# Attention with routed keys and an FFN: rounding the weights on VectorE alone, checking them in a second reading, and running the second block a few turns behind

## The chip, the cores and the metric

One core of a Trainium2 chip runs the kernel. The metric is device time in microseconds; for the kernel before, the median of three runs is 1088.34 us (1087.57 to 1089.61). Engines are named as the profile names them: PE is TensorE, PEld its weight load, DVE is VectorE, ACT is ScalarE, POOL is GpSimd, SP is the queue that issues the DMAs.

## The reference

Two blocks follow each other. The first is an attention with 4 batches, 8 heads, 768 positions and head size 64: each query and each key is given to the nearest of 16 centroids of its head, and a query attends only to keys of the same cluster. The second is an FFN on 3072 tokens with 512 inputs and 2048 hidden units.

```python
mask = q_assign[:, :, :, None] == k_assign[:, :, None, :]
scores = scale * np.matmul(q, k.transpose(0, 1, 3, 2))
scores = np.where(mask, scores, -1000000000.0)
attn = np.exp(scores - max); attn = attn / (attn.sum(-1) + 1e-09)   # in short
x = np.matmul(attn, v)            # (B,H,S,D) -> (B*S, H*D)
# ...
h = x @ w_in                      # 512 x 2048
g = h * (1.0 / (1.0 + np.exp(-1.702 * h)))
out = (g @ w_out).astype(np.float32)   # 2048 x 512
```

The FFN's weights come in as 64-bit floats: two 32-bit words for each number. The kernel reads them as words and makes 32-bit floats of them itself.

## The kernel before

The main loop has 96 turns (and two more to drain). A turn `t` works on two units of attention: scores (PE), for the first batch a matmul on one-hot clusters (`part`), `exps` (ACT), `mask` (DVE for the later batches, and the sums on POOL), and the `values` (PE) of the turn before. Twelve turns make half a batch, 24 a batch. Every third turn normalises a group; the fourth of these releases the FFN of that half batch, 28 chunks: 16 `first` (x times w_in, then tanh on ACT, then a product on DVE) and 12 `second` parts (g times w_out). Chunks are handed out by the turn.

The weights are 32 chunks of 128 x 512 numbers, 512 KB each as they come. Chunk by chunk they are rounded into `w_in` (16 chunks) and then `w_out` (16).

```python
def load_w(i):                       # SP; the raw words, three buffers
    if i < NW:
        t = wp.tile([P, WN, 2], I32, name="raw")
        nc.sync.dma_start(out=t.rearrange("p n t -> p (n t)"), in_=w_chunks[i][1])
        w_raw[i] = t

def split_w(i):                      # hi: the high words, every second one
    hi = w_raw[i][:, :, 1]; w = w_chunks[i][0]
    e = wp.tile([P, WN], I32, name="e")
    nc.vector.tensor_scalar(out=e, in0=hi, scalar1=EXP, scalar2=None, op0=ALU.bitwise_and)   # L159
    nc.vector.tensor_scalar(out=w.bitcast(I32), in0=hi, scalar1=0xFFFFF, scalar2=None,
                            op0=ALU.bitwise_and)                                             # L161
    nc.scalar.activation(out=e, in_=e, func=AF.Relu, scale=8.0, bias=low[:, 0:1])            # L163
    nc.scalar.activation(out=w, in_=w.bitcast(I32), func=AF.Copy, scale=2.0 ** -20, bias=1.0)# L165
    w_pow[i] = e

def join_w(i):
    raw, e, w = w_raw.pop(i), w_pow.pop(i), w_chunks[i][0]
    nc.vector.scalar_tensor_tensor(out=e, in0=raw[:, :, 1], scalar=-2 ** 31, in1=e, ...)     # L171
    nc.vector.scalar_tensor_tensor(out=w, in0=raw.bitcast(U32)[:, :, 0], scalar=2.0 ** -52,
                                   in1=w, op0=ALU.mult, op1=ALU.add)                         # L174
    nc.vector.tensor_tensor(out=w, in0=w, in1=e.bitcast(FP32), op=ALU.mult)                  # L177

def round_next():                    # splits a chunk, joins the one before
    i = w_done[0]
    if i < NW:
        load_w(i + 2)
        split_w(i)
    if 0 < i <= NW:
        join_w(i - 1)
    w_done[0] += 1
```

Normalising and its check, and the FFN:

```python
def normalise(g):
    sm = sum_of.pop(g); ps = bank()               # bank(): one of three PSUM banks
    # ... two pairs of matmuls with ones            L453
    rec = recs[g] = short()
    nc.vector.reciprocal(out=rec, in_=ps[:, 0:HALF])                                         # L456
    x = xT_of[g] = O_of.pop(g)
    nc.vector.tensor_tensor(out=x, in0=x, in1=rec, op=ALU.mult)                              # L458
    if g % HP == HP - 1:
        ffn.extend(ffn_chunks(g // HP))

def check(g):                        # ACT sums 1/sum, to see whether it is in range
    rec = recs.pop(g)
    nc.scalar.activation(out=rec, in_=rec, func=AF.Copy, accum_out=sums[:, 0, g:g + 1])      # L468
    nc.scalar.activation(out=rec, in_=rec, func=AF.Relu, ...)                                # L470

def first(f):
    round_to((f * P // WN + 1) * NCH)             # rounds what it needs, here and now
    ps = bank()
    # ... matmuls                                   L487
    g = hs[f] = gp.tile([P, HALF], FP32, name="g")
    nc.scalar.activation(out=g, in_=ps[:, 0:HALF], func=AF.Tanh, scale=0.851)                # L492
    nc.vector.scalar_tensor_tensor(out=g, in0=g, scalar=1.0, in1=ps[:, 0:HALF], ...)         # L494
```

The loop (TB is 24, a batch):

```python
rate = (NF + NH * (NF // 4)) / (TB / 2 - 0.5)
for t in range(NT + 2):
    # scores (L384), part (L398), exps (L409) of two units
    second = t >= TB // 2
    if second:
        round_next()
    # mask (L420; sums L430); prep_near (L276); values (L441) of the turn before
    owed = owed + rate if ffn else 0.0
    # normalise(g) in every third turn, other preparation of the next heads
    # (transposes L262, assignment L287-L316), check
    if second or t and t % 4 != 3:
        round_next()
    while owed >= 1 and ffn:
        ffn.popleft()()
        owed -= 1
    if second and t % 2:
        round_next()
# after the loop: the chunks that are left, and a flag for a fallback kernel
```

If a sum or a weight is out of range, a flag sends the work to a second, general kernel, which does not run with these inputs.

Of the kernel before, what the change touches and what calls it, by code (L numbers as in the profile page):

```python
# [2 lines left out]

# [35 lines left out]
def fast(  # L39
# [21 lines left out]
    nc = tc.nc  # L61
# [26 lines left out]
    xp = ctx.enter_context(tc.tile_pool(name="xp", bufs=HP + 2))  # L88
# [63 lines left out]
    EXP = 0x7FF00000  # L152

    def split_w(i):

        hi = w_raw[i][:, :, 1]
        w = w_chunks[i][0]
        e = wp.tile([P, WN], I32, name="e")
        nc.vector.tensor_scalar(out=e, in0=hi, scalar1=EXP, scalar2=None,  # L159
                                op0=ALU.bitwise_and)  # L160
        nc.vector.tensor_scalar(out=w.bitcast(I32), in0=hi, scalar1=0xFFFFF,  # L161
                                scalar2=None, op0=ALU.bitwise_and)
        nc.scalar.activation(out=e, in_=e, func=AF.Relu, scale=8.0,  # L163
                             bias=low[:, 0:1])
        nc.scalar.activation(out=w, in_=w.bitcast(I32), func=AF.Copy,  # L165
                             scale=2.0 ** -20, bias=1.0)
        w_pow[i] = e

    def join_w(i):
        raw, e, w = w_raw.pop(i), w_pow.pop(i), w_chunks[i][0]  # L170
        nc.vector.scalar_tensor_tensor(  # L171
            out=e, in0=raw[:, :, 1], scalar=-2 ** 31, in1=e,
            op0=ALU.bitwise_and, op1=ALU.bitwise_or)
        nc.vector.scalar_tensor_tensor(  # L174
            out=w, in0=raw.bitcast(U32)[:, :, 0], scalar=2.0 ** -52, in1=w,
            op0=ALU.mult, op1=ALU.add)
        nc.vector.tensor_tensor(out=w, in0=w, in1=e.bitcast(FP32),  # L177
                                op=ALU.mult)

    w_done = [0]  # L180

    def round_next():
        i = w_done[0]
        if i < NW:
            load_w(i + 2)
            split_w(i)
        if 0 < i <= NW:
            join_w(i - 1)
        w_done[0] += 1

    def round_to(n):
        while w_done[0] <= min(n, NW):
            round_next()
# [11 lines left out]
    low = const.tile([P, 1], FP32, name="low")  # L205
    nc.vector.memset(low, -896.0 * 2.0 ** 23)
# [10 lines left out]

    hot = const.tile([P, NJ * 4, 32], BF16, name="hot")
    nc.vector.memset(hot, 0.0)
    sums = const.tile([P, 2, 2 * NPAIR], FP32, name="sums")  # L220

# [829 lines left out]
```

## Time and profile before

| | before |
|---|---|
| median of three runs | 1088.34 us |
| span of the profiled run | 1087.3 us |
| mean granted TensorE clock | 0.990 |
| HBM read, written | 38.04 MB, 6.31 MB |
| POOL sums (L430), 160 of them | 1840 ns (128 of them) and 1876 ns (32) each |
| DVE masks (L420), 288 | 609 ns each |
| DVE reciprocals (L456), 32 | 2551 ns each |

How to read it: a line of the profile's groups gives the kernel's line, engine, operation, what it writes and reads with shapes, how often, busy time and mean duration, and the idle time before it with what ended that. A busy share is an average over the span; a turn of the main loop can be found in the timeline by its scores matmuls (L384).

### The profile page before, as it was taken

The page shows a single profiled execution, that of the slowest core. Times are in us where ns is not written, and L with a number is a line of the kernel's source. Part 1 is how long each engine was busy: PE and PEld are TensorE (multiplying, and loading weights), DVE is VectorE, ACT ScalarE, POOL GpSimd, SP SyncE. Part 2 cuts the span into 40 slices and gives each one's busy share as a digit, 9 for nine tenths or more (in the row PEclk, how much of TensorE's full clock was granted, in tenths as well). Part 3 has the DMA queues.
Part 4 walks back from the last instruction along what each step waited for, and adds up shares of the span by engine and source line. Part 5 has one row for each costly group of instructions (what it writes and reads, how often), then busy time and mean ns, then how long its engine had stood idle before and what let it go on. Part 6 is the DMA issues. An engine that isn't in the chain of part 4 may idle for free. (4 is left out here: it accounts for less than half of the span.)

```text
span 1087.3 us, 10456 instructions
## 1 busy us (share of the span) xinstructions
PE 1049.0 (96%) x3982; PEld 492.6 (45%) x3982; DVE 490.8 (45%) x744; ACT 354.8 (33%) x665; POOL 296.9 (27%) x168
## 2 busy tenths in 40 slices
PE   7878799999999999999999999999999999999997
PEld 3423344445544455444454445444554445444543
DVE  3889999225442344424453164423552344431200
ACT  3755555223422333223432233223332133311100
POOL 2644223213232333123231142222332333230000
PEclk9998899999999999999999999999999999999999
DMA  7623443110100010002100000010000000000000
GB/s 199 165 81 116 131 133 111 46 49 17 49 23 27 10 30 15 31 25 54 51 23 17 15 20 15 15 48 32 8 7 12 10 10 1 1 10 20 1 11 22
DMA packets 64813, 45.13 MB, mean 42 GB/s; under 512 B 51953, under 2 KB 57585, under 8 KB 64753
## 3 DMA queue, kind: packets, MB, share of 16 engines
q1 hardware_dynamic: 64608, 44.33, 14.3%
q8 instruction: 33, 0.54, 0.2%
q14 instruction: 28, 0.22, 0.1%
q10 hardware_dynamic: 144, 0.03, 0.0%
HBM read 38.04 MB, written 6.31 MB: 41 GB/s over the span
## 5 line engine op out<-in xcount | busy, mean ns | idle before, releaser
L430 POOL TENSOR_TENSOR sum<-sum,A 128x768 f32<-128x768 f32 x128 | 235.5, 1840 | 461.3 <-DVE A L420 364.1
L487 PE MATMUL m<-x,w_in 128*128 128x384 f32 x1024 | 347.1, 494 | 9.7 <-ACT T L267 4.4
L504 PE MATMUL m<-w_out,g 128*128 128x512 f32 x768 | 337.8, 594 | 0.7 <-ACT short L282 0.7
L420 DVE SCALAR_TENSOR_TENSOR A<-qb,code,s 128x384 f32<-128x384 uint8 x288 | 157.6, 609 | 274.6 <-ACT s L409 251.9
L487 PEld LDWEIGHTS m<-x,w_in 128*128 128x128 f32 x1024 | 192.2, 192 | 149.1 <-issue 16.3
L504 PEld LDWEIGHTS m<-w_out,g 128*128 128x128 f32 x768 | 143.3, 190 | 175.6 <-issue 171.5
L494 DVE SCALAR_TENSOR_TENSOR g<-g,m 128x384 f32<-128x384 f32 x128 | 70.0, 553 | 220.4 <-ACT g L492 220.3
L384 PE MATMUL s<-T,T 64*128 64x384 f32 x768 | 152.9, 517 | 9.7 <-ACT A L409 9.6
L409 ACT ACTIVATE s<-s 128x768 f32<-128x768 f32 x144 | 107.9, 792 | 136.0 <-PE s L384 136.0
L441 PE MATMUL o<-A,inv 128*64 128x384 f32 x768 | 146.3, 502 | 0.0
L492 ACT ACTIVATE g<-m 128x384 f32<-128x384 f32 x128 | 61.7, 487 | 196.4 <-PE m L487 196.3
L430 POOL TENSOR_TENSOR sum<-A 128x768 f32<-128x768 f32 x32 | 60.0, 1876 | 215.6 <-DVE A L420 179.5
L384 PEld LDWEIGHTS s<-T,T 64*128 64x128 f32 x768 | 66.6, 189 | 94.6 <-issue 52.2
L456 DVE RECIPROCAL short<-m 128x384 f32<-128x384 f32 x32 | 81.6, 2551 | 25.8 <-PE m L453 25.8
L441 PEld LDWEIGHTS o<-A,inv 128*64 128x64 f32 x768 | 46.8, 137 | 84.8 <-issue 84.1
L510 ACT ACTIVATE y<-m 128x512 f32<-128x512 f32 x24 | 14.3, 595 | 155.8 <-PE m L504 142.7
L468 ACT ACTIVATE short<-short 128x384 f32<-128x384 f32 x32 | 16.7, 523 | 111.2 <-DVE x L458 111.2
L409 ACT ACTIVATE A<-s 128x768 f32<-128x768 f32 x48 | 36.1, 804 | 22.0 <-PE s L398 22.0
L267 ACT COPY T<-m 128x384 f32<-128x384 f32 x64 | 29.7, 480 | 37.2 <-PE m L262 37.1
L262 PE MATMUL m<-ident,in 128*128 128x128 f32 x192 | 33.9, 298 | 3.1 <-ACT T L267 1.7
L163 ACT ACTIVATE e<-e,low 128x512 int32<-128x512 int32 x32 | 23.1, 722 | 28.8 <-DVE e L159 28.8
L262 PEld LDWEIGHTS m<-ident,in 128*128 128x128 f32 x192 | 21.5, 146 | 22.4 <-issue 11.9
(68 smaller groups left out, 373.5 us busy)
## 6 DMA issues: line engine op xcount, KB each, us to landing
raw<-in_moe_w_in_dram SPq DMA_DIRECT2D x16, 512.0 KB
raw<-in_moe_w_out_dram SPq DMA_DIRECT2D x16, 512.0 KB
in<-in_q_dram SPq DMA_DIRECT2D x32, 192.0 KB
in<-in_k_dram SPq DMA_DIRECT2D x32, 192.0 KB
inv<-in_v_dram SPq DMA_DIRECT2D x16, 384.0 KB
out_dram<-y SPq DMA_DIRECT2D x24, 256.0 KB
qb<-line SPq DMA_DIRECT2D x12, 192.0 KB
line<-row SPq DMA_DIRECT2D x12, 1.5 KB
```

What stands on the lines that cost most here:

```text
L262: nc.tensor.transpose(out=ps[:, n * P:(n + 1) * P], in_=qk_in[p, w][:, h * NH + n].rearrange("p a d -> p (a d)"), identity=ident)
L267: nc.scalar.copy(dst, ps[:, 0:HALF])
L384: nc.tensor.matmul(out=ps[:, a, 0:HALF], lhsT=T[p, 1][rows, kt * P:(kt + 1) * P], rhs=T[p, 0][rows, h * HALF:(h + 1) * HALF], start=True, ...
L409: nc.scalar.activation(out=A_of[u] if p < HP else s, in_=s, func=AF.Exp, scale=SCALE)
L420: nc.vector.scalar_tensor_tensor(out=A_of[u][:, a, :], in0=qcode[p][:, a, h * HALF:(h + 1) * HALF], scalar=code[p][:, kt % NH, 1, kt // NH ...
L430: nc.gpsimd.tensor_tensor(out=sum_of[g], in0=A_of[u - 1] if kt == 1 else sum_of[g], in1=A, op=ALU.add)
L441: nc.tensor.matmul(out=o_of[g][a * D:(a + 1) * D, 0:HALF], lhsT=v_in[p][:, a, kt, :], rhs=A[:, a, :], start=(kt == 0), stop=(kt == NJ - 1))
L456: nc.vector.reciprocal(out=rec, in_=ps[:, 0:HALF])
L487: nc.tensor.matmul(out=ps[:, 0:HALF], lhsT=w_in[:, c, f * P:(f + 1) * P], rhs=xT[c], start=(c == 0), stop=(c == NCH - 1))
L492: nc.scalar.activation(out=g, in_=ps[:, 0:HALF], func=AF.Tanh, scale=0.851)
L494: nc.vector.scalar_tensor_tensor(out=g, in0=g, scalar=1.0, in1=ps[:, 0:HALF], op0=ALU.add, op1=ALU.mult)
L504: nc.tensor.matmul(out=ps[:, 0:DM], lhsT=hs[f][:, n * P:(n + 1) * P], rhs=w_out[:, f, :], start=(f == 0), stop=(f == NF - 1))
```

## The change

Three things change. First, a chunk's rounding is one chain of five VectorE operations: the high word shifted left by three and masked, the top two bits put back, the exponent taken out as a power of two, the low word multiplied into its place and added. ScalarE has no part in it, and a call of `round_next` does a whole chunk. The shift loses exponent bits of numbers out of the 32-bit range, so the range is checked apart: each chunk's raw words are fetched a second time, from turn 31 on in every odd turn, and four VectorE operations and one on ScalarE count what lies outside. Second, rounding is spread over turns 0 to 24, and FFN chunks no longer call for rounding themselves: each carries the number of rounded chunks that it needs and waits in its queue for it. Third, up to turn 24 the FFN is handed out at 28/16 chunks a turn, afterwards at 28/12, and it keeps a backlog from half batch to half batch; a seventh x buffer allows for it. It is for a steadier load at the start, where rounding, attention and the FFN's first chunks meet.

```diff
--- before.py
+++ after.py
# cut: an import, a constant that is no longer used, blank lines
@@ -85,7 +87,7 @@
     asg = ctx.enter_context(tc.tile_pool(name="asg", bufs=2))
     tmp = ctx.enter_context(tc.tile_pool(name="tmp", bufs=3))
     ap = ctx.enter_context(tc.tile_pool(name="ap", bufs=4))
-    xp = ctx.enter_context(tc.tile_pool(name="xp", bufs=HP + 2))
+    xp = ctx.enter_context(tc.tile_pool(name="xp", bufs=2 * HP - 1))
     gp = ctx.enter_context(tc.tile_pool(name="gp", bufs=NF))
     yp = ctx.enter_context(tc.tile_pool(name="yp", bufs=2))
     dram = ctx.enter_context(tc.tile_pool(
@@ -149,48 +151,58 @@
-    EXP = 0x7FF00000
-    def split_w(i):
-        hi = w_raw[i][:, :, 1]
-        w = w_chunks[i][0]
-        e = wp.tile([P, WN], I32, name="e")
-        nc.vector.tensor_scalar(out=e, in0=hi, scalar1=EXP, scalar2=None,
+    ODD = -2 ** 30
+    POWER = -2 ** 23
+    rounded, checked = [0], [0]
+    def round_next():
+        i = rounded[0]
+        if i == NW:
+            return
+        load_w(i + 2)
+        raw, w = w_raw.pop(i), w_chunks[i][0]
+        e = wp.tile([P, WN], I32, name="e", bufs=2)
+        hi, lo, w_i = raw[:, :, 1], raw.bitcast(U32)[:, :, 0], w.bitcast(I32)
+        nc.vector.tensor_scalar(out=w_i, in0=hi, scalar1=3, scalar2=0x3FFFFFF8,
+                                op0=ALU.logical_shift_left,
+                                op1=ALU.bitwise_and)
+        nc.vector.scalar_tensor_tensor(out=w_i, in0=hi, scalar=ODD, in1=w_i,
+                                       op0=ALU.bitwise_and, op1=ALU.bitwise_or)
+        nc.vector.tensor_scalar(out=e, in0=w_i, scalar1=POWER, scalar2=None,
                                 op0=ALU.bitwise_and)
-        nc.vector.tensor_scalar(out=w.bitcast(I32), in0=hi, scalar1=0xFFFFF,
+        nc.vector.scalar_tensor_tensor(
+            out=e.bitcast(FP32), in0=lo, scalar=2.0 ** -52,
+            in1=e.bitcast(FP32), op0=ALU.mult, op1=ALU.mult)
+        nc.vector.tensor_tensor(out=w, in0=w, in1=e.bitcast(FP32), op=ALU.add)
+        rounded[0] += 1
+    LEAST, MOST = (np.uint32(n).view(np.float32).item()
+                   for n in (897 << 20, (1151 << 20) - 1))
+    def check_next():
+        i = checked[0]
+        if i == NW:
+            return
+        if i == 0:
+            load_w(0)
+        if i + 1 < NW:
+            load_w(i + 1)
+        hi = w_raw.pop(i)[:, :, 1]
+        e = wp.tile([P, WN], I32, name="e", bufs=2)
+        nc.vector.tensor_scalar(out=hi, in0=hi, scalar1=0x7FFFFFFF,
                                 scalar2=None, op0=ALU.bitwise_and)
-        nc.scalar.activation(out=e, in_=e, func=AF.Relu, scale=8.0,
-                             bias=low[:, 0:1])
-        nc.scalar.activation(out=w, in_=w.bitcast(I32), func=AF.Copy,
-                             scale=2.0 ** -20, bias=1.0)
-        w_pow[i] = e
-    def join_w(i):
-        raw, e, w = w_raw.pop(i), w_pow.pop(i), w_chunks[i][0]
-        nc.vector.scalar_tensor_tensor(
-            out=e, in0=raw[:, :, 1], scalar=-2 ** 31, in1=e,
-            op0=ALU.bitwise_and, op1=ALU.bitwise_or)
-        nc.vector.scalar_tensor_tensor(
-            out=w, in0=raw.bitcast(U32)[:, :, 0], scalar=2.0 ** -52, in1=w,
-            op0=ALU.mult, op1=ALU.add)
-        nc.vector.tensor_tensor(out=w, in0=w, in1=e.bitcast(FP32),
-                                op=ALU.mult)
-    w_done = [0]
-    def round_next():
-        i = w_done[0]
-        if i < NW:
-            load_w(i + 2)
-            split_w(i)
-        if 0 < i <= NW:
-            join_w(i - 1)
-        w_done[0] += 1
-    def round_to(n):
-        while w_done[0] <= min(n, NW):
-            round_next()
+        hi, e = hi.bitcast(FP32), e.bitcast(FP32)
+        nc.vector.tensor_scalar(out=e, in0=hi, scalar1=LEAST, scalar2=MOST,
+                                op0=ALU.max, op1=ALU.min)
+        nc.vector.tensor_tensor(out=e, in0=hi, in1=e, op=ALU.not_equal)
+        nc.vector.scalar_tensor_tensor(out=e, in0=hi, scalar=0.0, in1=e,
+                                       op0=ALU.not_equal, op1=ALU.mult)
+        nc.scalar.activation(out=e, in_=e, func=AF.Copy, scale=2.0 * LIMIT,
+                             accum_out=sums[:, 2, i:i + 1])
+        checked[0] += 1
     load_qk(1, 0)
     load_v(0)
@@ -217,7 +227,8 @@
     hot = const.tile([P, NJ * 4, 32], BF16, name="hot")
     nc.vector.memset(hot, 0.0)
-    sums = const.tile([P, 2, 2 * NPAIR], FP32, name="sums")
+    sums = const.tile([P, 3, NW], FP32, name="sums")
+    assert NW == 2 * NPAIR
@@ -481,7 +493,6 @@
         def first(f):
-            round_to((f * P // WN + 1) * NCH)
             ps = bank()
             for c in range(NCH):
                 nc.tensor.matmul(out=ps[:, 0:HALF],
@@ -496,7 +507,6 @@
                                            op1=ALU.mult)
         def second(n, part):
-            round_to(NW // 2 + 4 * (part + 1))
             if part == 0:
                 ys[n] = bank()
             ps = ys[n]
@@ -512,8 +522,10 @@
                     out=out[b * S:(b + 1) * S, :].rearrange(
                         "(p j) n -> p j n", j=NJ)[:, h * NH + n, :], in_=y)
-        return ([lambda f=f: first(f) for f in range(NF)]
-                + [lambda n=n, part=part: second(n, part)
+        return ([((f * P // WN + 1) * NCH, lambda f=f: first(f))
+                 for f in range(NF)]
+                + [(NW // 2 + 4 * (part + 1),
+                    lambda n=n, part=part: second(n, part))
                    for n in range(NH) for part in range(NF // 4)])
@@ -545,8 +557,7 @@
         if i in (1, 3) and loads:
             load_qk(*loads.popleft())
-    rate = (NF + NH * (NF // 4)) / (TB / 2 - 0.5)
-    owed = 0.0
+    owed, n_ffn = 0.0, NF + NH * (NF // 4)
     for p, i in [(0, i) for i in range(6)] + [(1, i) for i in range(2)]:
         prep(p, i)
         if p == 0 and i in (1, 3):
@@ -562,7 +573,7 @@
         for u in us:
             exps(u)
         second = t >= TB // 2
-        if second:
+        if second or t == 0:
             round_next()
         for u in us:
             mask(u)
@@ -572,7 +583,11 @@
         if 1 <= t <= NT:
             for u in range(2 * t - 2, 2 * t):
                 values(u)
-        owed = owed + rate if ffn else 0.0
+        if not ffn:
+            owed = 0.0
+        else:
+            owed += n_ffn / (TB / 2 if t > TB else 16)
         g = (t - 2) // TG if t >= 2 and (t - 2) % TG == TG - 1 else None
         if g is not None and second:
             normalise(g)
@@ -582,22 +597,25 @@
             normalise(g)
         if recs:
             check(*recs)
-        if second or t and t % 4 != 3:
+        if not second:
             round_next()
-        while owed >= 1 and ffn:
-            ffn.popleft()()
+        while owed >= 1 and ffn and ffn[0][0] <= rounded[0]:
+            ffn.popleft()[1]()
             owed -= 1
         if second and t % 2:
             round_next()
-    ok = const.tile([P, 2, 2 * NPAIR], FP32, name="ok")
+        if t >= TB + TB // 4 and t % 2:
+            check_next()
+    ok = const.tile([P, 3, NW], FP32, name="ok")
     nc.vector.tensor_scalar(out=ok, in0=sums, scalar1=LIMIT, scalar2=None,
                             op0=ALU.is_le)
     ok1 = const.tile([P, 1], FP32, name="ok1")
     nc.vector.tensor_reduce(out=ok1, in_=ok, axis=AX.XY, op=ALU.min)
     for _ in range(NF // 2):
-        ffn.popleft()()
+        ffn.popleft()[1]()
     ps = bank()
     nc.tensor.transpose(out=ps[0:1, 0:P], in_=ok1, identity=ident)
     okt = const.tile([1, 1], FP32, name="okt")
@@ -606,7 +624,7 @@
     nc.vector.tensor_scalar(out=bad, in0=okt, scalar1=-1.0, scalar2=1.0,
                             op0=ALU.mult, op1=ALU.add)
     while ffn:
-        ffn.popleft()()
+        ffn.popleft()[1]()
         if len(ffn) == 4:
             is_bad = nc.values_load(bad[0:1, 0:1], min_val=0, max_val=1)
     return is_bad
```

## Prediction

> **What bounds the kernel now.** I read the page first, then busy time by stretch, then TensorE's waits, then the timelines. From the page (part 1, and slices of part 2; 40 slices of 27 us):
>
> ```profile
> PE 1049.0 (96%) x3982; PEld 492.6 (45%) x3982; DVE 490.8 (45%) x744; ACT 354.8 (33%) x665; POOL 296.9 (27%) x168
> ...
> PE   7878799999999999999999999999999999999997
> ...
> DVE  3889999225442344424453164423552344431200
> ...
> PEclk9998899999999999999999999999999999999999
> ```
>
> TensorE is full except in the first seven slices, and there VectorE (DVE) is what is full. I cut the trace by turn (a turn starts with its first scores matmul): turns 0-11 are 11.85-82.10 us, turns 12-16 end at 138.43, turn 24 ends at 229.57. Columns: stretch, length, busy PE, weight load, DVE, ACT, POOL, granted clock, DMA share, GB/s.
>
> ```profile
> 11.85:82.10 70.25, 57.90 (x380) 25.50 (x379) 51.01 (x75) 42.22 (x80) 34.90 (x18) 0.97 0.51 139
> 82.10:138.43 56.33, 45.52 (x168) 20.14 (x168) 54.45 (x69) 28.70 (x52) 20.90 (x10) 0.85 0.41 125
> 138.43:229.57 91.14, 90.12 (x347) 41.10 (x346) 57.69 (x86) 38.79 (x71) 24.43 (x13) 1.00 0.29 85
> 229.57:1087.30 857.73, 849.12 (x3061) 402.06 (x3060) 324.60 (x500) 241.16 (x457) 215.25 (x119) 1.00 0.07 21
> ```
>
> In turns 12-16 DVE is busy 54.5 of 56.3 us while TensorE idles 10.8 and its mean clock is 0.85. After turn 24 TensorE is the bound; of the 8.6 us idle there, about 6 are the last output's way out. So only turns 0-24 have much to give. TensorE's waits between 30 and 140 us (total, times, longest):
>
> ```profile
> PE s L384 <- ACT A L409: 9.6, 5, 4.0
> PE m L487 <- ACT T L267: 4.1, 1, 4.1
> PE m L487 <- DVE g L494: 2.9, 1, 2.9
> PE m L487 <- DVE x L458: 2.4, 1, 2.4
> ```
>
> All lead to DVE's queue. The scores wait for ACT's exps; ACT's queue stood at L468 (which reads what DVE's reciprocal makes) or at L163/L165 (which read DVE's split of a weight chunk). The FFN waits for x or g behind rounding ops.
>
> For prices I take a clean stretch (TensorE's timeline at 909-937 us):
>
> ```profile
> 908.49 1.56 PE L384 MATMUL s<-T,T 64*128 64x384 f32 x8
> ...
> 916.78 1.56 PE L384 MATMUL s<-T,T 64*128 64x384 f32 x8
> ...
> 927.65 1.56 PE L384 MATMUL s<-T,T 64*128 64x384 f32 x8
> ...
> 936.59 1.56 PE L384 MATMUL s<-T,T 64*128 64x384 f32 x8
> ```
>
> These turns hold two, three and two `first` chunks: 8.29, 10.87 and 8.94 us. So a `first` is 2.58 us, attention alone 8.29 - 5.16 = 3.13, a normalisation 0.65 (the third turn has one). The turn after (to 948.31) has two `first` and one `second` part: 3.43 for that. In block 0 the one-hot matmuls add 0.50.
>
> **Turns 0-24 by these prices.** Turns 12-24: 13 x 3.63 less 0.5 (turn 24 has no one-hots) = 46.7; four normalisations 2.6; transposes and prep 3.1; 16 `first` 41.3; 10 `second` parts 34.3; sum 128.0. They took 147.5 (82.10 to 229.57), so 19.5 are lost. Turn 11 took 7.49 for 3.63: 3.9 lost. Turns 0-10 took 62.8 for some 52.4: 10.4 lost, about a third of it start-up. About 34 us in all: TensorE's idle time, and a clock of 0.50 in three windows (81.49-88.32, 115.63-119.04, 129.28-136.11, 17.1 us together), each around a wait.
>
> **What the Trainium skill says.** "TensorE: Matmul & The Clock Gate", section What's actually happening: the clock falls to half after an idle window of about 3.4 us. The trace agrees: the 4.0, 2.9 and 4.1 us waits stand beside those windows, whose lengths are one or two times 3.41. "SBUF — State Buffer", section SBUF: two separate sides: DVE (two-port mode, or two SBUF inputs) and GpSimd take an exclusive lock on a port pair for a whole instruction. The trace agrees: L161 took 0.42 us alone and up to 2.05 beside a sum on POOL, which averages 1.84 us. "VectorE: DVE Perf Modes", section The perf-mode tier table: an fp32 tensor_scalar from SBUF runs at 2x, a tensor_tensor at 1x. At 128x512, 0.42 against 0.69 us agrees, so I price the new ops by kind.
>
> **The change: rounding.** One clean chunk now, on DVE's timeline:
>
> ```profile
> 111.26 0.42 DVE L159 TENSOR_SCALAR e<-raw 128x512 int32<-128x512 int32 x1
> 111.60 0.42 DVE L161 TENSOR_SCALAR w_in<-raw 128x512 int32<-128x512 int32 x1
> 111.93 0.68 DVE L171 SCALAR_TENSOR_TENSOR e<-raw,e 128x512 int32<-128x512 int32 x1
> 112.54 0.69 DVE L174 SCALAR_TENSOR_TENSOR w_in<-raw,w_in 128x512 f32<-128x512 uint32 x1
> 113.26 0.69 DVE L177 TENSOR_TENSOR w_in<-w_in,e 128x512 f32<-128x512 f32 x1
> ```
>
> Start to start this is 0.34 + 0.33 + 0.61 + 0.72 + 0.61 = 2.61 us (the next op starts at 113.87). The new chain is again two tensor_scalar, two scalar_tensor_tensor and one tensor_tensor on the same shapes: 2.61, nothing saved on DVE. By the groups' means (0.60 + 0.67 + 0.79 + 0.84 + 0.97 = 3.87 against 2.90 clean) collisions with POOL add 0.97, so I reckon 3.6 us a chunk, before and after. Removed are ACT's two ops, 0.72 + 0.61 = 1.33 us a chunk, 43 us in all: ACT is only 33% busy, but no longer stands in line for DVE's split.
>
> **Spreading.** Before, 8 rounds by turn 11, then 2.5 a turn plus those the FFN forced, done by turn 21. After: two in turn 0, one in turns 1-11, then 1.5 a turn, 32 by turn 24. The FFN gets 1.75 chunks a turn up to turn 24: 19 by its end in place of 26. The seven left are `second` parts, 24.0 us moved later, not saved. Then 28/12 = 2.33 a turn; the gate on rounded chunks never closes (17 rounded when four are needed, 30 when 20 are).
>
> Turns 12-24 after: TensorE 128.0 - 24.0 = 104.0. DVE: 19 rounds x 3.6 = 68; four normalisations x 3.1 (2.55 + 0.56) = 12; 16 g x 0.55 = 9; an assignment 2.3; the masks of turn 24 2.4: 94. DVE now fits, at 90%. I leave 5 for the wait for x before the first chunk and the like: 109. Gain 147.5 - 24.0 - 109 = 14.5.
>
> Turns 0-11: DVE gets five more rounds, 18 us, on 51 busy of 70. Its idle time before (15.2-23.4, 65.9-69.4, and shorter ones) takes most, so TensorE runs about as now. The waits behind L468 lose the 1.33 us that ACT rounded in, about 1 us in each of three; I take 2.5 in all.
>
> **The second reading.** From turn 31 in odd turns: 0.34 + 0.34 + 0.61 + 0.61 = 1.9 us on DVE (3.5 with collisions) and 0.8 on ACT (0.61 + 0.19), 32 times; 16.8 MB where the DMA share is 0.07. No wait for weights: each is fetched a check ahead, but for the first. In line it does delay: the last g of a turn ends 1.05 us into the next, the check 1.9 later, and ACT's sum of it keeps the next exps from 0.8 until 3.7, so masks end near 7 in place of 4. The shortest following turn with two FFN chunks is 8.3 us, so the scores' buffers come free in time. Where the turn also normalises or prepares, ACT's late copies can hold a bank 1-2 us. I add 3.
>
> Sum: 1088.3 - 14.5 - 2.5 + 3 = 1074.3.
>
> **Rivals.** (1) The check becomes the wait: ACT stands still up to 3 us in 32 turns. If TensorE lost 1 us each time, 1103 at the 32 and no gain net. For it: ACT is in order and already stands 111 us at L468 in all. Against: TensorE ran without a gap right through that. (2) DVE is the bound in turns 0-11: rounds 13 x 3.5 = 45, assignments 13, normalisations 9.5, together 67.5 from 15.2 us on, hence to 82.7, all of what turns 0-11 have now. Any wait in that queue delays exps; half the gain goes: about 1082. (3) All 34 us come back but start-up: about 1056. It needs DVE never to lag, and at 90-100% that is unlikely. (4) DMA hides nothing either way: same time as without it.
>
> **Range and chances.** The early gain is 8 to 26, the check 0 to 9: 1063 to 1086. Faster by over 2% (below 1066.6) needs 22 us net, two thirds of all that is lost: 0.14. Slower by over 2% needs the first rival in full: 0.03.
>
> **What would show it.** Right: turn 24 ends near 188 us (229.6 - 24.0 - 17); DVE is near 90% from 15 to 190 us and has no long full stretch with TensorE idle; the clock's half windows after 80 us fall from 17 us to below 7; 19 FFN chunks lie before turn 25; ACT is some 17 us less busy (43 less 32 x 0.8). Wrong: new TensorE gaps in even turns after 32, released by ACT's exps or DVE's masks; waits for x or exps of over 3 us in turns 4-13; DVE ops of another price than 2.61 a chunk.

## The result, and the profile after

The changed kernel takes **1117.99 us** (median of four runs, 1117.22 to 1118.68); the kernel before takes 1088.72 on the same chip (four runs). The ratio is 1.0269, with an interval of 1.0252 to 1.0287: slower by 29 us, where 1074.3 was predicted and 1086 was the top of the range.

The page of the kernel after, parts 1 and 2:

```profile
span 1116.1 us, 10657 instructions
...
PE 1056.1 (95%) x3982; PEld 495.3 (44%) x3982; DVE 592.7 (53%) x871; ACT 336.7 (30%) x665; POOL 297.5 (27%) x168
...
PE   7687789999999999999999999999999999999997
...
DVE  5799989943555536544466345644375445520200
...
PEclk9798889999999999999999999999999999999999
```

Look at the first eight slices. VectorE stands at 8 or 9 from the third to the eighth, so the load is steady, as the change means it to be. TensorE is no fuller there than before (7687789 against 7878799) and its clock is lower. VectorE was given more to do and TensorE got nothing for it.

Busy time by stretch, kernel after: turns 0-11, turns 12-24, and the rest (columns as in the prediction: stretch, length, busy PE, weight load, DVE, ACT, POOL, granted clock, DMA share, GB/s).

```profile
13.38:103.13 89.75, 65.11 (x380) 28.20 (x380) 78.50 (x92) 33.99 (x63) 35.64 (x18) 0.87 0.46 133
103.13:227.16 124.03, 108.75 (x457) 50.06 (x457) 113.71 (x135) 38.35 (x73) 43.34 (x22) 0.94 0.33 94
227.16:1116.10 888.94, 874.58 (x3117) 412.41 (x3116) 396.90 (x630) 260.23 (x523) 217.17 (x120) 1.00 0.13 40
```

- Turns 0-11 take 89.75 us in place of 70.25, with the same 380 matmuls.
- Turns 12-24 take 124.0 in place of 147.5. But 56 matmuls fewer lie there (457; before, 168 + 347 = 515, give or take a record): seven `second` parts, which the prediction prices at 24.0.
- Turn 24 therefore ends at 227.16, before at 229.57: only 2.4 us earlier although a good 24 us of TensorE's work has been put off. After it the kernel needs 888.9 us in place of 857.7, or 31.2 more: 25.5 more of busy PE (874.58 - 849.12) and 5.7 more of idle time. 31.2 - 2.4 is the 28.8 by which the two spans differ.

What TensorE lost before turn 25 can be estimated from these lines as its idle time plus half of its busy time in the windows whose granted clock is 0.50. The sums over these windows, four in the kernel before and then six in the kernel after (length, then busy time of each engine):

```profile
sum 20.48, PE 19.03 PEld 8.39 DVE 16.90 ACT 9.80 POOL 10.09; mean PE 4.76 PEld 2.10 DVE 4.22 ACT 2.45 POOL 2.52
sum 37.57, PE 27.11 PEld 12.76 DVE 31.50 ACT 10.35 POOL 5.64; mean PE 4.52 PEld 2.13 DVE 5.25 ACT 1.72 POOL 0.94
```

After: 24.6 + 15.3 idle and 13.6 by the clock, together 53.5. Before, with the idle time of the prediction's lines: 12.4 + 11.8 idle and 9.5 by the clock, 33.7, which agrees with the "34 us in all" that the prediction drew from its price list. So the change set out to win back these 34 us, and lost 20 more. The 20 are all lost in turns 0-11 (33.8 in place of 14.1). Turns 12-24, where 14.5 were to be won, lose 19.7 as against 19.6.

TensorE's waits of the kernel after between 13 and 227 us (line that waits, who ended the wait; total, times, longest):

```profile
PE m L360 <- DVE hot L319: 8.0, 2, 4.1
PE m L498 <- DVE x L469: 7.7, 1, 7.7
PE m L273 <- DVE qb L365: 6.7, 2, 4.8
PE m L334 <- DVE qc L327: 6.5, 1, 6.5
PE m L498 <- DVE g L505: 3.4, 3, 2.4
```

Before, the longest item was the scores waiting for ScalarE's exps (9.6 us). Now the five longest items are all VectorE's: one-hots (`hot`), centroid products (`qb`, `qc`), `x` and `g`, each behind rounding in VectorE's queue. Those for `hot`, `qb` and `qc` fall in turns 2 to 10, that for `x` in turn 14.

### The profile page after: what moved, and what is told of

It is laid out like the page before. It is cut to its first block, busy times and chain, and to the rows that moved or that the text cites. A ratio compares the mean times of both kernels' runs of the same rounds, so it can differ in the third digit from the quotient of the medians.

```text
span 1116.1 us, 10657 instructions
## 1 busy us (share of the span) xinstructions
PE 1056.1 (95%) x3982; PEld 495.3 (44%) x3982; DVE 592.7 (53%) x871; ACT 336.7 (30%) x665; POOL 297.5 (27%) x168
## 3 DMA queue, kind: packets, MB, share of 16 engines
HBM read 54.82 MB, written 6.31 MB: 55 GB/s over the span
## 5 line engine op out<-in xcount | busy, mean ns | idle before, releaser
L395 PE MATMUL s<-T,T 64*128 64x384 f32 x768 | 156.0, 526 | 3.8 <-ACT A L420 2.7
L273 PE MATMUL m<-ident,in 128*128 128x128 f32 x192 | 36.5, 312 | 12.5 <-DVE qb L365 6.7
L203 ACT ACTIVATE e<-e 128x512 f32<-128x512 f32 x32 | 20.1, 629 | 73.4 <-DVE e L201 73.4
```

The costliest lines, as they stand in the source:

```text
L273: nc.tensor.transpose(out=ps[:, n * P:(n + 1) * P], in_=qk_in[p, w][:, h * NH + n].rearrange("p a d -> p (a d)"), identity=ident)
L395: nc.tensor.matmul(out=ps[:, a, 0:HALF], lhsT=T[p, 1][rows, kt * P:(kt + 1) * P], rhs=T[p, 0][rows, h * HALF:(h + 1) * HALF], start=True, ...
```

## Experiments

All ratios are to the kernel before, run on the same chip, with 95% intervals. The expectations were on record before each run. Because the main loop's turns can be found in every trace, the most telling number is often when turn 24 ends; what follows it depends mostly on how much FFN is left and on whether there is a second reading. The kernel before has medians of 1087.9 to 1088.7 us on the chips used, so a difference between runs of two chips is good to about 1 us.

| kernel | turn 11 ends | turn 24 ends | from there to the end |
|---|---|---|---|
| before | 82.10 | 229.57 | 857.7 |
| after | 103.13 | 227.16 | 888.9 |
| e1: new chain alone | 91.44 | 244.11 | 857.8 |
| e8: new FFN pace alone | 81.81 | 216.64 | 883.5 |
| e2: pace and rounding slots, old chain | 89.66 | 212.34 | 883.5 |
| e3: all but the second reading | 104.91 | 228.21 | 883.5 |

### The parts, one at a time

**e1, the new chain alone.** In the kernel before, `split_w` and `join_w` are replaced; slots, FFN pace and flag stay, and there is no second reading.

```diff
-            split_w(i)
-        if 0 < i <= NW:
-            join_w(i - 1)
+            chain_w(i)        # the five VectorE operations of the change
```

> The new chain alone: the kernel before, with its own turns for rounding, its forced rounds and its FFN pace, but each chunk rounded by the five VectorE operations; no second reading. Theory A (the chain itself costs: each of its operations waits for the one before, 2.97 us start to start in place of 2.61, and it meets GpSimd's sums more often, 1.66 us a chunk in place of 0.97): 12 us from the pace and up to 22 from collisions on a VectorE that is full in turns 11 to 21, less what ScalarE no longer delays: 1095 to 1108. Theory B (the slots of the rounding are to blame, the chain is harmless): 1080 to 1090.

Measured: 1103.57 us, 1.0143 (1.0126 to 1.016), 15.2 slower. All of it lies before turn 25 (14.5 later there, then 857.8 as before). A chain that I took to cost VectorE the same costs half of the whole loss.

**e2, the schedule alone.** The change's slots, FFN pace and x buffers, with the old split and join and no second reading.

```diff
# against the kernel after, in short
-def round_next():             # the new chain
+def round_next():             # split of chunk i, join of chunk i - 1, as before
-        while owed >= 1 and ffn and ffn[0][0] <= rounded[0]:
+        while owed >= 1 and ffn and ffn[0][0] <= rounded[0] - 1:
-        if t >= TB + TB // 4 and t % 2:
-            check_next()
```

> The new schedule alone: the kernel after with the old split and join (two operations on ScalarE), two buffers for the exponents, no second reading. Its turns for rounding and its FFN pace are those of the kernel after. Theory A (chain): 1072 to 1082, the gain that the prediction saw. Theory B (13 chunks by turn 11 in place of 8 stand in VectorE's queue ahead of what prepares the next heads): 1095 to 1110.

Measured: 1097.62, 1.0087 (1.007 to 1.0104), 9.2 slower. The spreading that was to gain over 14 loses by itself.

**e3, all but the second reading.**

```diff
-        if t >= TB + TB // 4 and t % 2:
-            check_next()
```

> The kernel after without the second reading of the weights (it leaves out their range check). If the time after turn 24 shows its cost rightly (a few waits of up to 1.5 us in even turns): 1111 to 1117. If the second reading were the cause of the loss: about 1088 or less.

Measured: 1112.23, 1.0218 (1.0201 to 1.0235). So the second reading costs 1117.99 - 1112.23 = 5.8 us, and 5.4 by the last column of the table. It is a small part of the loss.

**e8, the FFN pace alone.** The old chain in its old slots (`round_to` is gone; a chunk waits for its weights), the new pace, no second reading.

```diff
# against the kernel after, in short; the chain and check_next as in e2
         owed, as in the change: 28/16 chunks a turn up to turn 24
-        if second or t == 0:
+        if second:
             round_next()
-        if not second:
+        if second or t and t % 4 != 3:
             round_next()
```

> The old split and join in the rounding slots of the kernel before (8 chunks by turn 11, then 2.5 a turn), with only the FFN's new pace: 1.75 chunks a turn up to turn 24, then 2.33, the gate in place of forced rounds, seven x buffers; no second reading. Theory S (in the schedule the early rounding slots cost, the pace is harmless or helps): 1078 to 1090. If the pace costs (work moved away from a TensorE that then idles): 1094 to 1100, as the whole schedule.

Measured: 1101.94, 1.0126 (1.0109 to 1.0143), 13.9 slower. Busy time by stretch of e8, turns 12-24 and the rest:

```profile
81.81:216.64 134.83, 115.29 (x457) 51.73 (x457) 119.45 (x155) 65.83 (x121) 44.17 (x23) 0.90 0.35 106
216.64:1100.10 883.46, 873.62 (x3117) 412.61 (x3116) 324.80 (x500) 243.00 (x459) 215.24 (x119) 1.00 0.07 21
```

This is the clearest table of the study. Seven `second` parts leave turns 0-24, and these end only 12.9 us earlier; the seven come back after turn 24, at 873.62 - 849.12 = 24.5 us of busy PE and 25.7 of time. Where TensorE waits for VectorE (119 us busy of 135), almost half of the work taken from it is not won: TensorE idles 19.5 us in place of 11.8, and its remaining work takes 4.1 longer, at a clock of 0.90 in place of 0.94. Before, VectorE's 155 operations were in the way of 26 FFN chunks, now of 19. Where TensorE is the bound, the same work costs its full time.

The four parts add up. Turn 24 ends 14.5 later by the chain, 12.9 earlier by the pace, 4.3 earlier by the rounding slots (e2 against e8: 212.34 - 216.64): 226.9, where the full change has 227.16. Then 25.7 for the moved work and 5.4 for the second reading. Some of this closeness is luck: turn 0 itself starts between 11.50 and 13.38 us in these runs, and counted from there the sum is 1.65 us off. The shares also hold in this order only, as e12 below shows.

### Why the chain is dear

VectorE's timeline of the kernel after, its first two chunks (start, duration):

```profile
16.69 0.41 DVE L167 TENSOR_SCALAR w_in<-raw 128x512 int32<-128x512 int32 x1
17.13 0.69 DVE L170 SCALAR_TENSOR_TENSOR w_in<-raw,w_in 128x512 int32<-128x512 int32 x1
17.86 0.43 DVE L172 TENSOR_SCALAR e<-w_in 128x512 int32<-128x512 int32 x1
18.32 0.69 DVE L174 SCALAR_TENSOR_TENSOR e<-raw,e 128x512 f32<-128x512 uint32 x1
19.05 0.69 DVE L177 TENSOR_TENSOR w_in<-w_in,e 128x512 f32<-128x512 f32 x1
19.66 2.04 DVE L167 TENSOR_SCALAR w_in<-raw 128x512 int32<-128x512 int32 x1
21.73 2.20 DVE L170 SCALAR_TENSOR_TENSOR w_in<-raw,w_in 128x512 int32<-128x512 int32 x1
23.96 1.92 DVE L172 TENSOR_SCALAR e<-w_in 128x512 int32<-128x512 int32 x1
```

The first chunk is clean, and takes 19.66 - 16.69 = 2.97 us where the old one took 2.61. The durations are the same 0.4 and 0.69. The starts are not: each operation reads what the one before it wrote, and starts 0.03 to 0.04 us after its end (17.13 + 0.69 = 17.82, next start 17.86). Only the sixth line is independent of the one ahead of it (a new chunk), and it starts 0.08 before that one's end. In the second chunk three operations in a row take about 2 us: a GpSimd sum stands beside each, as GpSimd's timeline shows:

```profile
19.38 2.03 POOL L441 TENSOR_TENSOR sum<-A 128x768 f32<-128x768 f32 x1 [15.56 <-ACT A L420]
21.54 4.06 POOL L441 TENSOR_TENSOR sum<-sum,A 128x768 f32<-128x768 f32 x2
```

So there are two costs: the order of the five, and more collisions with these sums. A chunk's mean durations sum to 3.87 us before, 4.16 in e1 and 4.57 after, against 2.90 clean. Of the 160 rounding operations 20 take over 1 us before, 26 in e1 and 35 after, and in these three traces every one of them has a sum on GpSimd running at some time of it.

**e6, two chunks interleaved.** The full change, but a call of `round_next` runs operations 1 to 3 of chunk i in turn with operations 4 and 5 of chunk i - 1, so that none reads its neighbour's result.

```diff
# in short
+        # order: op1(i), op4(i-1), op2(i), op5(i-1), op3(i)
-        while owed >= 1 and ffn and ffn[0][0] <= rounded[0]:
+        while owed >= 1 and ffn and ffn[0][0] <= rounded[0] - 1:
```

> The kernel after with two chunks' chains interleaved, so that no rounding operation follows the one whose result it reads. Theory D (the 0.10 to 0.12 us more between starts is the wait for the operation before): starts go back to 2.61 us a chunk, 11 us less for VectorE, and 1104 to 1110. If the pace belongs to the operations themselves, not to their order: no change of pace, 1114 to 1120.

Measured: 1103.08, 1.013 (1.0111 to 1.0149), 14.9 less than the full change. VectorE's timeline of e6:

```profile
97.26 0.42 DVE L168 TENSOR_SCALAR w_in<-raw 128x512 int32<-128x512 int32 x1
97.60 0.69 DVE L174 SCALAR_TENSOR_TENSOR e<-raw,e 128x512 f32<-128x512 uint32 x1
98.20 0.69 DVE L178 SCALAR_TENSOR_TENSOR w_in<-raw,w_in 128x512 int32<-128x512 int32 x1
98.80 0.69 DVE L182 TENSOR_TENSOR w_in<-w_in,e 128x512 f32<-128x512 f32 x1
99.40 0.42 DVE L185 TENSOR_SCALAR e<-w_in 128x512 int32<-128x512 int32 x1
99.74 0.42 DVE L168 TENSOR_SCALAR w_in<-raw 128x512 int32<-128x512 int32 x1
```

The same five operations now start 0.34, 0.60, 0.60, 0.60 and 0.34 apart: 2.48 a chunk. The mean durations fall from 4.57 to 4.12 as well.

**e16, the interleaved chain in the kernel before** (its slots and its pace, no range check at all).

```diff
-            split_w(i)
-        if 0 < i <= NW:
-            join_w(i - 1)
# in short
+        # order: op1(i), op4(i-1), op2(i), op5(i-1), op3(i)
```

> The kernel before with the new chain interleaved over two chunks, in its own slots and at its own FFN pace; no second reading, so the range of the weights is not checked. If the chain's cost was its order alone: 2.48 us a chunk in place of the old 2.61, ScalarE out of the line, and 1080 to 1089, against 1103.6 for the same chain in one piece. If VectorE-only rounding costs for another reason too: 1095 to 1104.

Measured: 1090.03, 1.003 (1.0003 to 1.0057). The chain's 15.2 us become 1.7. That is still not a gain, although a chunk's mean durations (3.76) are a little below those before and ScalarE has no part in it. Busy time by stretch of e16, turns 0-11 and 12-24:

```profile
11.86:88.50 76.64, 59.51 (x381) 25.79 (x380) 53.40 (x73) 33.93 (x64) 36.30 (x18) 0.91 0.45 126
88.50:229.65 141.15, 133.35 (x514) 61.30 (x514) 105.37 (x156) 40.07 (x75) 59.69 (x23) 0.95 0.35 105
```

Turns 12-24 are 6.3 us shorter than before (141.15 against 147.47), and turns 0-11 give it back: 76.64 against 70.25, with two waits of TensorE for `qb` (3.3 and 5.0 us; before, one of 1.4). The sums are also longer: GpSimd is busy 59.7 us with its 23 instructions in turns 12-24, against 45.3 with 23 in the kernel before, and one sum takes 8.3 us where the longest before takes 3.2.

**e5, the full change with fewer GpSimd sums.** Of five sums for each group of the first batch (turns 0-23) one is left, so the normalisation is left out in substance, and the flag is a constant.

```diff
+        if p < HP and kt > 1:
+            return
         nc.gpsimd.tensor_tensor(out=sum_of[g], ...)
```

> The kernel after without most of GpSimd's sums in the first batch's turns 0 to 23 (four of five are left out, so the first batch is normalised by a part of its sums; the flag for the fallback is left out too). Theory L (the lock on the port pair: each sum holds one rounding operation up by about 1.5 us): the five operations fall from 4.57 us a chunk to about 2.95 at the mean, 50 us less for VectorE, and most of it reaches the end, because VectorE is the bound there: 1075 to 1090. If collisions fill time that VectorE would wait anyway: 1108 to 1118.

Measured: 1077.52, 0.9913 (0.9891 to 0.9934): 40 us less than the full change. Groups of VectorE by line, first of the kernel after and then of e5 (busy, mean ns, idle before):

```profile
L170 DVE SCALAR_TENSOR_TENSOR w_out<-raw,w_out 128x512 int32<-128x512 int32 x16 | 20.2, 1263 | 0.5
L177 DVE TENSOR_TENSOR w_in<-w_in,e 128x512 f32<-128x512 f32 x16 | 19.0, 1186 | 0.5
```

```profile
L170 DVE SCALAR_TENSOR_TENSOR w_out<-raw,w_out 128x512 int32<-128x512 int32 x16 | 11.1, 693 | 0.5
L177 DVE TENSOR_TENSOR w_in<-w_in,e 128x512 f32<-128x512 f32 x16 | 11.1, 692 | 0.5
```

**e14, the kernel before with the same sums left out** (and the same constant flag).

```diff
+        if p < HP and kt > 1:
+            return
-    nc.vector.tensor_scalar(out=ok, in0=sums, scalar1=LIMIT, scalar2=None, op0=ALU.is_le)
+    nc.vector.memset(ok, 1.0)
```

> The kernel before without four of five of GpSimd's sums in the first batch (the flag for the fallback left out too). It prices the lock in the old kernel and is the base for the next run. Theory L (lock): the old chain falls from 3.87 to about 2.95 us a chunk, some 30 us of VectorE's time, and the 20 us that TensorE waits in turns 11 to 16 mostly go: 1060 to 1072. If the lock matters only for the new chain: 1080 to 1088.

Measured: 1074.46, 0.9866 (0.985 to 0.9883), 13.8 less. Leaving these sums out is worth 14 us in the kernel before and 40 in the kernel after. Rounding operations of over 1 us fall from 20 to 3 and from 35 to 4. GpSimd's own time goes as well, but in turns 0-24 no engine of the kernel before waits for a sum, and after it is ScalarE alone that waits a notable time, 2.5 us; so what the sums cost there, they cost mostly by way of VectorE's queue. These kernels (e5, e14 and e15) leave work out and are no candidates.

**e15, the new pace with the sums left out:** e8 with the edit of e14.

```diff
         # on e8: pace of the change, slots and chain of before
+        if p < HP and kt > 1:
+            return
```

> The run with the new FFN pace alone, and again without those sums. Theory P (the pace costs 13.6 us because it takes TensorE's work out of turns that VectorE bounds and puts it behind them, where TensorE is the bound): with VectorE relieved the pace loses most of its cost, and this run lies within 5 us of the one before it, 1060 to 1076. If the pace costs by itself (the backlog, the later turns): 12 to 15 us above it.

Measured: 1080.43, 0.9922 (0.9905 to 0.9939): 6.0 above e14, where the pace cost 13.9 with the sums. Turns 12-24 of e14, and then of e15:

```profile
81.08:215.92 134.84, 129.89 (x514) 58.99 (x514) 92.34 (x155) 66.95 (x123) 9.80 (x5) 0.99 0.37 109
```

```profile
81.25:196.73 115.48, 107.79 (x458) 49.25 (x458) 93.91 (x155) 65.05 (x121) 9.20 (x5) 0.96 0.41 123
```

With VectorE relieved to 92 us, TensorE is busy 129.9 of 134.8 in e14, and putting off the seven parts brings turn 24 forward by 19.2 us (215.92 to 196.73) in place of 12.9. This supports the explanation of e8: the moved work is recovered as far as TensorE doesn't wait for VectorE in the stretch that it leaves. The expectation was missed, though, if by little: the run was to lie within 5 us of e14 and below 1076. VectorE is still busy 94 of 115 us in e15, so part of the bound may remain; the last 6.0 us I didn't take apart further.

### Slots and places in the queue

**e4, fewer rounds early:** the full change with the 8 rounds of the kernel before in turns 0-11.

```diff
-        if second or t == 0:
+        if second:
             round_next()
-        if not second:
+        if not second and t and t % 4 != 3:
             round_next()
```

> The kernel after, with the rounding slots of the kernel before in turns 0 to 11 (8 chunks: none in turn 0, 3, 7 and 11); later as in the kernel after, so that the last chunk is rounded in turn 27. Theory B (too many rounds early): turns 0 to 11 fall from 90 us back to 72 to 76, in all 1095 to 1104. Theory A (the chain's price): turns 0 to 11 gain the 5 x 4.6 us of work less, but turns 12 to 27 give most of it back: 1108 to 1116.

Measured: 1114.70, 1.0247 (1.023 to 1.0264), 3.3 less than the full change. Turn 24 ends 15.6 earlier (211.58), and nearly all is given back: rounding runs on into turn 27, FFN chunks wait for their weights, turn 28 takes 37.1 us, and masks stand behind rounding. TensorE's waits in e4, 211 to 320 us:

```profile
PE s L395 <- DVE A L431: 8.8, 3, 4.6
```

From turn 24 to the end e4 takes 900.7 us, 11.8 more than the full change: 5.4 more of idle time (the three waits are 8.8; other idle time is less) and 6.4 more of busy PE, some 3.5 of it one more `second` part (18 FFN chunks lie before turn 25, not 19).

**e7, the old chain with fewer early rounds:** e2 with e4's early slots and two rounds a turn in turns 12-17.

```diff
-        if not second:
+        if not second and t and t % 4 != 3:
             round_next()
-        if second and t % 2:
+        if second and (t % 2 or t < 18):
             round_next()
```

> The old split and join, 8 chunks by turn 11 as in the kernel before, then 2 a turn up to turn 17 and 1.5 after, done by turn 25; the FFN's new pace; no second reading. A candidate for a version better than both. If early slots are what the schedule loses by: turns 0 to 11 take 70 us, turns 12 to 24 some 115: 1080. If VectorE's total load in turns 0 to 24 sets the time however it is spread: 1088 to 1096.

Measured: 1093.38, 1.0048 (1.0031 to 1.0065). Of the kernels with the new pace and all of the attention's work this is the fastest, and the old chain needs no second reading; still the pace costs more (13.9 in e8) than the slots bring (8.6 from e8 to e7).

**e12, the full change at nearly the old pace** (28/11.5 chunks a turn throughout).

```diff
-            owed += n_ffn / (TB / 2 if t > TB else 16)
+            owed += n_ffn / (TB / 2 - 0.5)
```

> The kernel after with the FFN pace of the kernel before (28/11.5 chunks a turn throughout; the gate on rounded chunks stays). The firsts come three turns earlier, but the gate holds the last second part of the first output until all 32 chunks are rounded in turn 24, so about as many chunks lie before turn 25 as in the kernel after. Theory P: little to win, as the same TensorE work ends up behind turn 24: 1110 to 1118. If the pace in itself were what costs: 1100 to 1106.

Measured: 1118.92, 1.029 (1.0268 to 1.0312), no difference from the full change. This doesn't contradict e8. The pace alone does not bring the chunks forward here, for rounding at 1.5 a turn doesn't feed them: turn 23 has no FFN chunk, and turn 24 takes 31.7 us with seven `second` parts in it. Undone together, and without the second reading, they leave e1's 1103.57.

**e17, the kernel before with all rounding at the end of the turn** from turn 12 on.

```diff
-        if second:
-            round_next()
...
-        if second and t % 2:
+        for _ in range((2 + t % 2) if second else 0):
             round_next()
```

> The kernel before with the same 2 or 3 rounds a turn from turn 12 on, but all of them after the turn's reciprocal and FFN chunks in VectorE's queue, none ahead of them. Theory Q (place in the queue: TensorE waits for reciprocals and g's that stand behind rounds): the waits of turns 12 to 16 shrink by 4 to 10 us, 1078 to 1085. Theory T (total load: VectorE is full there, and it does not matter which work goes first): 1086 to 1091.

Measured: 1088.99, 1.0013 (1.0006 to 1.002). TensorE's waits in e17 between 30 and 140 us:

```profile
PE s L384 <- ACT A L409: 11.6, 5, 4.0
PE m L487 <- ACT T L267: 3.1, 1, 3.1
```

The waits of the FFN for `x` and `g` (2.4 and 2.9 us before) are gone from the list, and the scores wait 11.6 in place of 9.6. Turns 12-24 of e17:

```profile
80.55:228.64 148.09, 136.42 (x513) 61.24 (x514) 98.63 (x155) 67.74 (x123) 43.05 (x23) 0.94 0.33 100
```

The place in the queue is all but indifferent. But VectorE is busy only 98.6 us here, in place of 112.1, with the same 155 operations (9 of the rounding operations take over 1 us, in place of 20), and the stretch is no shorter than the 147.47 before. So VectorE's busy time does not set these turns by itself; what TensorE waits for in VectorE's queue, and when, counts as well.

**e18, the full change with rounding last** from turn 12 on.

```diff
-        if second or t == 0:
+        if t == 0:
             round_next()
-        if second and t % 2:
+        for _ in range((1 + t % 2) if second else 0):
             round_next()
```

> The kernel after with the rounds of turns 12 to 24 behind the turn's reciprocal and FFN chunks, none ahead. Theory Q: the 7.7 us wait for x in turn 14 and those for g and the reciprocal in turns 17 to 23 shrink, 1106 to 1113. Theory T: 1115 to 1120, as in the kernel after.

Measured: 1114.90, 1.0248 (1.0233 to 1.0263): 3.1 less than the full change, a tenth of the loss.

**e19, e17 with the interleaved chain** and no range check.

```diff
         # on e17: slots at the end of the turn
+        # order: op1(i), op4(i-1), op2(i), op5(i-1), op3(i)
```

> The interleaved new chain in the kernel before's number of rounds a turn and FFN pace, with the rounds behind the turn's critical work from turn 12 on; no second reading. Theory Q: 1076 to 1086 and the best of all. Theory T: 1087 to 1092, as with the rounds in their old places.

Measured: 1092.96, 1.0047 (1.003 to 1.0064), no better than e16. None of the orders tried got below the kernel before. None of the kernels that do the whole of the work beat it.

### The second reading

TensorE's waits in the kernel after, 300 to 1000 us:

```profile
PE m L498 <- ACT row L339: 3.1, 2, 1.5
PE m L273 <- ACT T L278: 1.7, 3, 0.6
PE s L395 <- DVE A L431: 0.9, 1, 0.9
PE m L273 <- ACT row L339: 0.7, 2, 0.3
```

The largest item is two waits of 1.5 us (turns 46 and 70), where ScalarE's late copy of a row holds a PSUM bank that the FFN needs: the mechanism that the prediction named ("ACT's late copies can hold a bank"). It and the 0.9 (turn 33) are absent from e3; the other two lines stand there too. After turn 24 the second reading costs 4.5 us of idle time and 0.9 of busy PE. The reading itself costs nothing in transfers: HBM reads rise from 38.04 to 54.82 MB, and no line of weights stands among the waits.

## Why the prediction was wrong, point by point

**The bound: right in the main.** TensorE is full except in turns 0-24, and what it waits for there leads to VectorE's queue; 34 us are lost. In e14 14 us come back when VectorE's rounding no longer meets the sums. That VectorE's busy time as such sets these turns is not shown; e17 speaks against it.

**The price of the rounding: the first step that failed.** "The new chain is again two tensor_scalar, two scalar_tensor_tensor and one tensor_tensor on the same shapes: 2.61, nothing saved on DVE", and "3.6 us a chunk, before and after". Pricing by kind left out who reads whom. The trace before showed it: the timeline that I quoted has 0.60 to 0.61 between independent operations and 0.72 where L177 reads what L174 has just made, and I added the 0.72 in without asking why it was longer. In place of 2.61 a clean chunk takes 2.97. With collisions, the old chunk's durations of 3.87 less its overlap (2.90 - 2.61) are 3.6, as predicted; the new one's 4.57 and its gaps (2.97 - 2.90) are 4.64. Over 32 chunks that is 33 us more of VectorE by these prices. "Before and after" failed for the old chain too: in e2, under the new schedule, its durations sum to 4.33 us a chunk in place of 3.87. e1 charges 15.2 us of time to the new chain, and e6 and e16 show that its order is the cause. The Trainium skill ("VectorE: DVE Perf Modes", section The DRAIN you can't avoid) says that an operation which isn't held starts before the pipe of the one ahead is empty, as the 0.60 after a duration of 0.69 shows here. That section puts no number on a reader of the last result; here it starts 0.10 to 0.13 us later than an independent operation.

**The schedule: the second step that failed, and the larger in the sum.** "The seven left are `second` parts, 24.0 us moved later, not saved", and then "Turns 12-24 after: TensorE 128.0 - 24.0 = 104.0 ... DVE now fits, at 90%", so 109 us. This credits a stretch that waits for VectorE with TensorE's time taken from it. Turns 12-24 took 124.0, with VectorE busy 113.7 in place of 94: its 19 rounds at 4.64 and not 3.6 are 20 us more. By e8 only 12.9 us came back for the moved work, against 25.7 paid later. In e5, where a chunk's durations sum to 3.11, turns 12-24 take 106.1 us and turn 24 ends at 185.9, so the predicted 109 and 188 do come with a cheap VectorE. The price of a part was a little low too: seven are 24.5 us of busy PE in e8, 3.5 each, where one turn had given 3.43.

**Turns 0-11: wrong in sign.** "DVE gets five more rounds, 18 us ... Its idle time before takes most, so TensorE runs about as now", with a gain of 2.5. They take 19.5 longer. VectorE's idle time there came in pieces in which it waited for others. Rival (2), which puts VectorE at its bound until 82.7, named the right engine and was 20 us short: turn 11 ends at 103.13, for its 13 rounds cost 4.64 and not 3.5 (15 us by these prices), and VectorE still idles 11 of the 89.75 us. With the sums left out (e5) turn 11 ends at 79.8.

**The second reading: mechanism right, size off.** Three us were added, 5.4 to 5.8 measured. Rival (1), which made it the wait at 32 us, fell. Rival (3) fell with the schedule (its 1056 should read 1058 to 1061, by the sums above it); rival (4) was right that the transfers are hidden. The range's top was also narrower than its parts: a gain of 8 and a check of 9 give 1089, not 1086.

**The signs that were named.** "Turn 24 ends near 188 us": 227. "The clock's half windows after 80 us fall from 17 us to below 7": they grew to 20.5. Windows of the kernel after at a clock of 0.50:

```profile
93.51:100.34 6.83, 5.40 (x19) 1.79 (x21) 6.58 (x10) 0.26 (x1) 0.00 (x0) 0.50 0.26 88
120.82:127.65 6.83, 3.42 (x8) 1.67 (x10) 6.59 (x7) 3.10 (x7) 1.68 (x1) 0.50 0.38 94
151.54:158.37 6.83, 5.36 (x9) 2.94 (x10) 5.86 (x6) 2.98 (x7) 3.96 (x2) 0.50 0.27 61
```

In each VectorE is busy for 5.9 to 6.6 of 6.83 us while TensorE, at half rate, is busy for 3.4 to 5.4. The idle window of about 3.4 us that the prediction cites for the clock is not borne out in full, though the prediction says that the trace agrees: the half window from 115.63 in the kernel before stands beside a wait of 2.9, the one from 151.54 here beside two of 1.5 and 2.4. "VectorE near 90%" was right (92% in turns 12-24, 87% in turns 0-11), but it was meant with TensorE full beside it. "19 FFN chunks lie before turn 25" and "ACT is some 17 us less busy" (354.8 to 336.7, 18.1) were right; the gate did not close. Of the signs of being wrong, "DVE ops of another price than 2.61 a chunk" appeared. Waits of over 3 us in turns 4-13 came too, but for `qb`, `hot` and `qc` (4.8, 4.1 and 6.5); the long one for `x` (7.7) came in turn 14, and none for exps was over 1.4.

The predicted sum was 1088.3 - 14.5 - 2.5 + 3. By the single runs it is +15 for the chain, +14 for the FFN pace, -4 for the rounding slots and +6 for the second reading: 31, where 29 was measured. The two steps that failed, the rounding's price and the schedule, hold nearly all of the miss.

What stays open: the last 6.0 us of the pace in e15; why e17, with 13.5 us less of busy VectorE, is no faster; and why the interleaved chain, with less VectorE time than the old split and join, gains nothing in the kernel before. Its loss lies in turns 0-11 with their waits for `qb`, and GpSimd's sums are longer in turns 12-24; that either is the cause was not tried.

## What to carry to other kernels

Putting work off helps only as far as its own engine is the bound: taken here from a stretch that waited for another engine, 24.5 us of work won 12.9 and cost 25.7 later. So ask first which engine is waited for in the stretch it leaves and in the one it enters. Price a chain of VectorE operations by start-to-start times of the same dependence, not by the kind of operation, and try two chains interleaved where each step reads the last. Where VectorE and GpSimd both work in SBUF, look for the operations that take longer beside the other engine's, and price a stretch with them: here the new chain in its new turns brought more of them (20, then 35), so a free share of VectorE was worth less than it looked.

## What the runs showed of the hardware that I had not expected

- On 128x512 words a VectorE operation that reads the result of the one just before starts 0.73 us after it (0.69 long) or 0.44 to 0.46 (0.42 long), in the kernel after; an independent one 0.60 and 0.34, in e6.
- What a chunk's five operations cost beside GpSimd depends on the kernel. 2.90 us clean, they average 3.87 (before), 4.16 (e1), 4.12 (e6), 4.57 (after) and 3.76 (e16) beside the same 160 sums; a 0.42 or 0.69 us operation can take 1.9 to 2.2, and a sum of 1.8 us up to 8.3 in e16. Leaving out four fifths of the first batch's sums was worth 13.8 us in one kernel and 40 in the other.
- Less busy time of VectorE is not less time: e17 has 13.5 us less of it in turns 12-24, and those turns take 148.1 us in place of 147.5.
